# Scores of one attention group and values of another in one TensorE visit, with the second batch's probabilities turned by DMA

## The chip, the cores and the metric

The kernel runs on one core of a Trainium2 chip. The metric is the device time of one execution in microseconds (us). All times below come from runs of the kernel before and from one profiled execution of it.

## What is computed

The inputs are q, k and v of 8 batches, 8 heads, 576 tokens and 64 values a head, and two weight matrices. Attention is sparse: in the first four heads a query sees the last 32 tokens, in the other four those tokens before it that stand at the same place modulo 32. A feed-forward layer with a gate follows.

```python
def _attn_ref(q, k, v):                      # B, H, S, D = 8, 8, 576, 64
    scores = (1 / np.sqrt(D)) * np.matmul(q, k.transpose(0, 1, 3, 2))
    rel = pos[:, None] - pos[None, :]
    mask_local = (rel >= 0) & (rel < 32)
    mask_strided = (rel >= 0) & (pos[None, :] % 32 == pos[:, None] % 32)
    masks = np.stack([mask_local if h < H // 2 else mask_strided for h in range(H)])
    attn = softmax(np.where(masks, scores, -1e9))
    return np.matmul(attn, v)

def _moe_ref(x, w_in, w_out):                # x: 4608 x 512, w_in: 512 x 2048, w_out: 2048 x 512
    h = x @ w_in
    return (h / (1 + np.exp(-h))) @ w_out
```

## The kernel before

**Work.** The 4608 tokens form nine blocks of 512. Blocks 0 to 2 go through the feed-forward layer in the plain way: for each of 16 chunks of 128 hidden channels one step `h` (`hidden`, L676, twelve wide matmuls of 128x128 by 512 columns into a bank of the PSUM ring `ph`), then tanh (ACT, L692), gate (DVE, L696), a split of the result into a rounded and a remaining part (L705, L709), then one step `o` (`output`, L725, twelve wide matmuls into four `po` banks). Every product is made of three, since values are split in two. Blocks 3 to 8 go in three pairs through a scheme with seven products in place of eight (L1482 for the first layer, L1521 for the second), which accumulate in three PSUM tiles of two banks, z0 to z2. A step `A` or `B` of it is again twelve wide matmuls.

**Attention** lies between these steps. Batch 0 has six groups of its own (c = 0 to 5); each later batch has three (c = 6 to 26), each of them a local group of 12 tiles and a strided one of 8 or 6. For a group the steps are: `S` (`scores`, L503: small matmuls of 64 rows in two passes, 72 or 80 records), `M` (DVE: mask and maximum, L531), `E` (ACT: exponentials, L540), `R` and `N` (DVE: sums and scaling), then the probabilities are turned, then `O` (`values`, L607: again 72 or 80 small matmuls) and `B` (`placed`, L627: ACT copies from PSUM to the activations x). In batches 0 and 1 they are turned on TensorE (`T`, `turn`, L564, with ACT's copies `P`, L575). From batch 2 on (`MOVED`, L105) they are turned by DMA: `X` copies the upper and the lower 16-bit halves of the words apart (`part`, L591), `Y` is one DMA transpose (`move`, L597), `Z` joins the halves (`join`, L603). Of the batches from 1 on, scores, transposes and values all take the one PSUM ring `pa` (two banks). There is one buffer `pt` for turned probabilities, so a group's first `X` or `P` waits for the values of the group before.

**Order.** Nothing in the instruction streams is ordered by a compiler. Each step has a cost per engine, the steps that it follows, the rings that it takes (`ready`, L253) and a due time; `arrange` (L264) goes through time and each moment starts the step with the smallest due time among those that could start, choosing the engine that would end first. Due times come from the order in which steps are added (`backward`), and two tables written by hand correct them (`SHIFT`) or fix the engine (`GIVEN`). The result is one fixed order for each engine; PE, SP (which issues all DMAs), DVE, ACT and POOL then wait for one another by semaphores alone. `plan` (L992) says beside which chunk of blocks 1 and 2 values, turning and scores of a group are added, 3.55 chunks for each group; `spread` (L1654) does the same for the first pairs. Loads of weights pass through six stage buffers and are rounded by ACT and DVE up to some 126 us.

Of the kernel before, what the change touches and what calls it, by code (L numbers as in the profile page):

```python
# [30 lines left out]
P = 128  # L31
# [43 lines left out]
class Group:  # L75
# [29 lines left out]
MOVED = 2  # L105
# [68 lines left out]
}  # L174
GIVEN = {
# [4 lines left out]
}  # L180
# [1578 lines left out]
```

## Time and profile before

| | us |
|---|---|
| median of 3 runs (lowest, highest) | 818.92 (816.71, 820.82) |
| the profiled execution | 815.51 |
| its span, first to last instruction | 813.7 |
| PE busy | 801.4 (98% of the span) |
| DVE busy | 563.2 (69%) |
| ACT busy | 498.6 (61%) |
| POOL busy | 4.7 (1%) |
| packets of the main DMA queue, share of 16 engines | 70.5% |

Shares of busy time are means over stages that differ, so the rows further down come by stage. PE is the matmul engine. Matmuls overlap and their ends are modelled, so differences of starts are safer than durations. A line number belongs to the kernel before.

### The profile page before, as it was taken

The page shows a single profiled execution, that of the slowest core. Times are in us where ns is not written, and L with a number is a line of the kernel's source. Part 1 is how long each engine was busy: PE and PEld are TensorE (multiplying, and loading weights), DVE is VectorE, ACT ScalarE, POOL GpSimd, SP SyncE. Part 2 cuts the span into 40 slices and gives each one's busy share as a digit, 9 for nine tenths or more (in the row PEclk, how much of TensorE's full clock was granted, in tenths as well). Part 3 has the DMA queues.
Part 4 walks back from the last instruction along what each step waited for, and adds up shares of the span by engine and source line. Part 5 has one row for each costly group of instructions (what it writes and reads, how often), then busy time and mean ns, then how long its engine had stood idle before and what let it go on. Part 6 is the DMA issues. An engine that isn't in the chain of part 4 may idle for free.

```text
span 813.7 us, 17555 instructions
## 1 busy us (share of the span) xinstructions
PE 801.4 (98%) x6920; PEld 656.1 (81%) x6920; DVE 563.2 (69%) x1382; ACT 498.6 (61%) x1176; POOL 4.7 (1%) x24
## 2 busy tenths in 40 slices
PE   6999999999999999999999999999999999999997
PEld 4888888888888888888888888888888888888886
DVE  6989887578888789822798776227976640379662
ACT  7998877355786748755787764564544344445440
POOL 2000000000000000000000000000000000000000
PEclk9999999999999999999999999999999999999999
DMA  8998796787876776776788777765555665555662
GB/s 321 324 309 277 256 259 221 213 264 224 241 215 216 229 221 236 262 237 230 261 247 255 275 242 263 215 200 192 194 205 196 233 243 176 201 207 185 209 225 105
DMA packets 107362, 188.85 MB, mean 232 GB/s; under 512 B 37648, under 2 KB 81680, under 8 KB 96528
## 3 DMA queue, kind: packets, MB, share of 16 engines
q1 hardware_dynamic: 107280, 187.74, 70.5%
q8 instruction: 54, 0.88, 0.4%
q14 instruction: 28, 0.23, 0.1%
HBM read 141.05 MB, written 38.80 MB: 221 GB/s over the span
## 4 chain that ended last, share of the span: by engine, by line
PE 97%; DVE 1%; DMA 1%; ACT 0%; issue 0%; SPq 0%; DVEq 0%
PE z L1482 28%; PE z L1521 28%; PE ph L682 17%; PE po L729 16%; PE pa L512 3%; PE pa L621 3%; DMA w<-kqt 1%; PE pa L569 0%; DVE osb L531 0%; PE po L621 0%; DVE sm L531 0%; DVE osb L548 0%; DVE osb L562 0%; DVE sums L557 0%; PE po L512 0%
## 5 line engine op out<-in xcount | busy, mean ns | idle before, releaser
L1482 PE MATMUL z<-w,w 128*128 128x512 f32 x720 | 167.1, 391 | 0.0
L1482 PEld LDWEIGHTS z<-w,w 128*128 128x128 f32 x720 | 134.5, 188 | 28.2
L1521 PE MATMUL z<-w,w 128*128 128x512 f32 x576 | 134.4, 390 | 0.0
L682 PE MATMUL ph<-xhi,w 128*128 128x512 f32 x384 | 127.8, 396 | 0.0
L1521 PEld LDWEIGHTS z<-w,w 128*128 128x128 f32 x576 | 107.8, 188 | 22.5
L540 ACT ACTIVATE sm<-sm,sums 128x64 f32<-128x64 f32 x304 | 101.7, 339 | 26.9 <-DVE sums L531 26.6
L729 PE MATMUL po<-w,g 128*128 128x512 f32 x432 | 103.7, 392 | 0.0
L729 PEld LDWEIGHTS po<-w,g 128*128 128x128 f32 x432 | 80.3, 188 | 17.0
L1348 DVE TENSOR_TENSOR w<-w,w 128x1024 fp32r<-128x1024 f32 (+3 forms) x68 | 77.5, 1151 | 11.1 <-ACT w L1419 9.4
L682 PEld LDWEIGHTS ph<-xhi,w 128*128 128x128 f32 x384 | 72.0, 188 | 15.9
L682 PE MATMUL ph<-xlo,w 128*128 128x512 f32 x192 | 74.8, 390 | 0.0
L1377 DVE TENSOR_TENSOR w<-w,z 128x1024 f32<-128x1024 f32 x30 | 36.5, 1219 | 43.2 <-PE z L1482 43.2
L1419 ACT CAST w<-w 128x1024 fp32r<-128x1024 f32 (+1 forms) x40 | 39.2, 987 | 32.9 <-PE z L1521 32.0
L540 ACT ACTIVATION_READ_ACCUMULATOR sm<-sm,sums 128x1 f32 x304 | 58.0, 191 | 0.0
L1365 ACT ACTIVATE w<-w 128x1024 f32<-128x1024 f32 x30 | 31.8, 1060 | 37.1 <-DVE w L1377 36.9
L1521 PE MATMUL z<-xhi,w 128*128 128x512 f32 x216 | 52.0, 390 | 0.0
L1521 PE MATMUL z<-xlo,w 128*128 128x512 f32 x216 | 52.0, 390 | 0.0
L1371 ACT COPY w<-z 128x1024 f32<-128x1024 f32 x30 | 30.4, 1013 | 34.7 <-PE z L1482 34.6
L1521 PEld LDWEIGHTS z<-xlo,w 128*128 128x128 f32 x216 | 40.5, 188 | 8.5
L1521 PEld LDWEIGHTS z<-xhi,w 128*128 128x128 f32 x216 | 40.5, 188 | 8.4
L692 ACT ACTIVATE th<-ph 128x512 f32<-128x512 f32 x48 | 28.5, 594 | 25.5 <-PE ph L682 13.5
L682 PEld LDWEIGHTS ph<-xlo,w 128*128 128x128 f32 x192 | 36.1, 188 | 6.9
(159 smaller groups left out, 1134.8 us busy)
## 6 DMA issues: line engine op xcount, KB each, us to landing
w<-ops SPq DMA_DIRECT2D x84, 1024.0 KB, 4.9
ops<-stage SPq DMA_DIRECT2D x48, 256.0 KB, 2.9
kd<-kqt SPq DMA_DIRECT2D x24, 448.0 KB, 5.1
ops<-w SPq DMA_DIRECT2D x80, 128.0 KB, 4.0
vd<-vt SPq DMA_DIRECT2D x24, 384.0 KB, 5.5
stage<-w_in SPq DMA_DIRECT2D x16, 512.0 KB, 6.2
stage<-w_out SPq DMA_DIRECT2D x16, 512.0 KB, 5.0
kd<-kqt SPq DMA_DIRECT2D x14, 442.0 KB, 4.6
```

Source lines behind the costliest of these rows:

```text
L512: nc.tensor.matmul(self.pss[rows, r, at : at + KW], kd[half, 1, g.q0[t] : g.q0[t] + g.rows], kd[half, 0, g.k0[t] : g.k0[t] + KW], start=Tr ...
L540: nc.scalar.activation(out=self.s_sb[:, c, r], in_=self.s_sb[:, c, r], func=AF.Exp, bias=self.nmax[:, c, r : r + 1], scale=-1.0, accum_out ...
L682: nc.tensor.matmul(ph, weight(0, wi, fc)[:, cc * P : (cc + 1) * P], x[xi][:, cc], start=(cc, n) == (0, 0), stop=(cc, n) == (NP - 1, 2),)
L692: nc.scalar.activation(out=th[:, cols], in_=ph[:, cols], func=AF.Tanh, scale=0.5)
L729: nc.tensor.matmul(po[tt], g[gi][:, cols], weight(1, wi, fc), start=fc == 0 and n == 0, stop=fc == NFC - 1 and n == 2,)
L1348: nc.vector.tensor_tensor(out=o, in0=x, in1=y, op=op1)
L1365: nc.scalar.activation(out=o, in_=x, func=AF.Silu)
L1371: nc.scalar.copy(out=o, in_=x)
L1377: nc.vector.tensor_add(o, x, y)
L1419: nc.scalar.copy(out=hi, in_=x)
L1482: nc.tensor.matmul(zt[z][:, jj], w[:, at, wi, cc * P : (cc + 1) * P], op[:, xi, cc], start=fresh and (cc, n) == (0, 0), stop=(cc, n) == (1 ...
L1521: nc.tensor.matmul(zt[zz][:, ds], w[:, at, wi, ds * P : (ds + 1) * P], op[:, gi, jj], start=fresh and (jp, jj, n) == (0, 0, 0), stop=(jp, ...
```

## The change

Five things are changed together:

1. From c = 9 to c = 24 the values of group c and the scores of group c + 2 are one step `V` for PE: first all of the scores, then all of the values, with nothing between them (`add_both`). These are 16 steps. Scores still go to `pa`. Values go to both banks of the ring `ph` in blocks 1 and 2 (nine steps), and to one of the tiles z0 to z2 in the first two pairs (seven steps). The last two groups keep a values step of their own.
2. Where values are in `ph`, ACT copies the local group in two instructions (one for each bank) in place of one.
3. Behind such a step in blocks 1 and 2 the output step of the same chunk is added at once.
4. `MOVED` is 1: batch 1 too is turned by DMA. Three `T` with their `P` go, three groups of `X`, `Y` and `Z` come.
5. `X` and `Z` may be done by POOL as well as by DVE or ACT; the planner chooses, and `GIVEN` names a few. Planned costs of these steps are other ones.

The tables `SHIFT` and `GIVEN` are new as a whole, and steps of one kind follow each other in the order of their chunks (`prior`).

```diff
-MOVED = 2
+MOVED = 1
...
-    copy = {"DVE": nc.vector.tensor_copy, "ACT": nc.scalar.copy}
+    copy = {"DVE": nc.vector.tensor_copy, "ACT": nc.scalar.copy, "POOL": nc.gpsimd.tensor_copy}
...
-        def values(self):
-            self.pso = self.bank("pso")
+        def values(self, ring=None):
+            if ring == "ph":
+                self.pso = [ps.tile([P, T], F32, name="ph") for _ in range(2)]
+            else:
+                at = pools["ps2"].tile([P, 2, T], F32, name=ring) if ring else self.bank("pso")
+                self.whole_pso, self.pso = at, [at[:, b] for b in range(2)]
...
+                if self.split:
+                    for b in range(2):
+                        nc.scalar.copy(
+                            out=flat[:, x0 + b * n : x0 + (b + 1) * n], in_=self.pso[b][:, base : base + n]
+                        )
+                    return
...
+    def add_both(c, ring):
+
+        a, s = groups[c], groups[c + 2]
+        a.split = ring == "ph"
+        add_keys(c + 2)
+        add_vs(c)
+
+        def go():
+            s.scores()
+            a.values(ring)
+
+        v = do(f"V{c}", {"PE": 2.68}, go,
+               reads=[f"kd{k}" for k in s.k] + [f"vd{v}" for v in a.v]
+               + [f"pt{c}.{i}" for i in range(len(a.gs))],
+               writes=[f"pss{c + 2}", f"pso{c}"], takes=[s.ring("pss")] + [ring] * (1 + a.split))
...
-                x = do(f"X{c}.{half}", {e: 0.1 + 0.13 * a.n for e in ("DVE", "ACT")}, lambda: None,
-                       reads=parts, writes=[f"half{c}.{half}"], due=after(0), takes=[] if half else [a.pt_from],
-                       after=[steps[f"X{c}.0"]] if half else [])
+                x = do(f"X{c}.{half}", {"POOL": 0.2 + 0.14 * a.n, "DVE": 0.06 + 0.08 * a.n, "ACT": 0.1 + 0.12 * a.n},
+                       lambda: None, reads=parts, writes=[f"half{c}.{half}"], due=after(0),
+                       takes=[] if half else [a.pt_from], after=[steps[f"X{c}.0"]] if half else before(c))
...
-        for what, c, at in (("V", i, 3.55 * i), ("T", i + 1, 3.55 * i + 1.2), ("S", i + 2, 3.55 * i + 2.4)):
+        for what, c, at in (("B", i, 3.55 * i), ("T", i + 1, 3.55 * i + 1.2)):
...
+                if plan[k, fc][0][0] == "B" and fc < NFC - 1:
+                    add_output(k, fc)
+                    put_out.add((k, fc))
...
-    for i, when in enumerate(((1, 2, 3), (4, 5, 6), (8, 9, 11), (13, 16, 18), (21, 23, 25), (29, 31, 33))):
-        spread(0, late + i, when)
-    for i, when in enumerate(((1, 2, 3), (5, 6, 7), (9, 10, 11))):
-        spread(1, late + 6 + i, when)
+    for i, when in enumerate(((2, 4, "z2"), (6, 8, "z1"), (10, 12, "z2"), (13, 16, "z0"), (20, 22, "z2"), (28, 30, "z1"))):
+        spread(0, late + i, *when)
+    for i, when in enumerate(((13, 15, "z2"), (21, 23), (29, 31))):
+        spread(1, late + 6 + i, *when)
```

## Rows read from the trace of the kernel before

**Rows 1.** table of stages: start:end, length, busy PE, PEld, DVE, ACT, POOL, clock, DMA share, GB/s

```profile
0.00:26.20 26.20, 18.18 (x485) 14.37 (x485) 18.71 (x110) 20.11 (x73) 4.74 (x24) 1.00 0.92 327
26.20:126.00 99.80, 99.80 (x1094) 81.48 (x1094) 89.97 (x279) 86.51 (x259) 0.00 (x0) 1.00 0.89 281
126.00:330.00 204.00, 204.00 (x2258) 165.63 (x2251) 165.99 (x553) 131.16 (x426) 0.00 (x0) 1.00 0.75 229
330.00:581.00 251.00, 251.00 (x2096) 205.79 (x2096) 153.55 (x316) 163.04 (x318) 0.00 (x0) 1.00 0.72 236
581.00:809.50 228.50, 228.46 (x1008) 188.88 (x1007) 133.73 (x126) 97.79 (x103) 0.00 (x0) 1.00 0.56 200
```

**Rows 2.** chain that ended last, in order of time: start us, us, what

```profile
140.10 1.32 PE pa L621 x80
...
156.62 2.72 PE ph L682 x12
...
217.06 1.32 PE pa L621 x80
```

**Rows 3.** timeline of PE around a scores visit: start us, us, line, operation, tiles, shapes

```profile
226.38 0.39 PE L682 MATMUL ph<-xhi,w 128*128 128x512 f32 x1
226.69 1.35 PE L512 MATMUL pa<-kd 64*32 64x64 f32 x80
227.97 0.50 PE L682 MATMUL ph<-xhi,w 128*128 128x512 f32 x1
...
228.54 0.40 PE L682 MATMUL ph<-xhi,w 128*128 128x512 f32 x1
```

**Rows 4.** groups by line, shapes apart: scores on 64x64 tiles; busy us, mean ns

```profile
L512 PE MATMUL pa<-kd 64*64 64x64 f32 x616 | 13.8, 225 | 0.0
```

**Rows 5.** timeline of PE around a values visit

```profile
124.11 0.84 PE L729 MATMUL po<-stage,g 128*128 128x512 f32 x3
124.89 1.39 PE L621 MATMUL pa<-pt,vd 64*64 64x32 f32 x80
...
126.54 0.40 PE L682 MATMUL ph<-xlo,w 128*128 128x512 f32 x1
```

**Rows 6.** timeline of PE in the opening, values ahead of scores

```profile
25.15 0.44 PE L621 MATMUL po<-th,w 64*64 64x54 f32 x13
25.83 0.44 PE L621 MATMUL po<-th,w 64*64 64x54 f32 x11 [0.24 <-issue]
```

**Rows 7.** page, DMA queues: packets, MB, share of 16 engines

```profile
q8 instruction: 54, 0.88, 0.4%
```

**Rows 8.** timeline of PE around the transposes of the first group of batch 1

```profile
39.66 0.39 PE L682 MATMUL ph<-xhi,w 128*128 128x512 f32 x1
39.90 0.93 PE L569 MATMUL pa<-ident,sm 128*128 128x128 f32 x7
...
41.12 0.40 PE L682 MATMUL ph<-xhi,w 128*128 128x512 f32 x1
```

**Rows 9.** instructions on tile pt: count, ns lowest/median/highest, first and last start us

```profile
L605 ACT COPY pt<-sm x23: 1059/1201/1225, 122.8 to 542.4; 128x896 uint16<-128x896 uint16 x16, 128x768 uint16<-128x768 uint16 x7
...
L595 DVE COPY pt<-sm x16: 554/620/628, 107.4 to 536.3; 128x896 uint16<-128x896 uint16 x10, 128x768 uint16<-128x768 uint16 x6
```

**Rows 10.** groups by line on POOL: busy us, mean ns

```profile
L368 POOL COPY mask_first<-mask_local 128x72 f32<-128x72 f32 x2 | 0.5, 238 | 0.1
```

**Rows 11.** DMA issues: count, median us from issue to landing

```profile
sm<-pt SPq DMA_TRANSPOSE x18, 4.5
```

**Rows 12.** timeline of ACT behind a values visit, ACT idle before

```profile
141.48 0.93 ACT L650 COPY xb<-pa 128x144 f32<-128x144 f32 x3 [2.76 <-PE pa L621]
142.19 0.54 ACT L633 COPY xb<-pa 128x384 f32<-128x384 f32 x1
```

**Rows 13.** timeline of ACT behind a values visit, ACT busy

```profile
223.72 0.54 ACT L633 COPY xb<-pa 128x384 f32<-128x384 f32 x1
```

**Rows 14.** timeline of ACT ahead of the first group turned by DMA

```profile
122.77 1.21 ACT L605 COPY pt<-sm 128x896 uint16<-128x896 uint16 x1
```

More of the change, by code (lines that the diff above doesn't have):

```diff
@@ L255, in ready @@
         at = 0.0
-        for ring in step.takes:
-            if len(self.taken[ring]) >= self.rings[ring]:
-                for other in self.taken[ring][-self.rings[ring]].ends[ring]:
+        for i, ring in enumerate(step.takes):
+            back = self.rings[ring] - step.takes[:i].count(ring)
+            if len(self.taken[ring]) >= back:
+                for other in self.taken[ring][-back].ends[ring]:
                     if other.end is None:
@@ L758, in sparse_attention_ffn, with add_keys @@
     outs_of = {}
+    def add_keys(c, after=lambda d: None):
+        a = groups[c]
+        for g, gi, k in zip(a.gs, a.gis, a.k):
+            cols = max(g.nq, g.nk)
+            do(f"k{c}.{gi}", {"SP": 2 * P * cols * 4 / QUICKER}, lambda gi=gi, k=k: load_qk(a.b, gi, k),
+               writes=[f"kd{k}"], due=after(-6))
+    def add_both(c, ring):
[10 more added lines that the diff above has]
+               writes=[f"pss{c + 2}", f"pso{c}"], takes=[s.ring("pss")] + [ring] * (1 + a.split))
+        both.append(v)
+        if not a.split:
+            late_steps.append(v)
+        add_peaks(c + 2, v)
+        take_values(c, v, ring)
+        add_total(c + 2)
+    both = []
     def add_scores(c, t0=None):
@@ L801, in add_total, with before @@
         steps.ends(steps[f"M{c}.0"], "sum", [r])
+    def before(c):
+        return [steps.by_name[n] for n in (f"O{c - 1}", f"V{c - 1}") if n in steps.by_name]
     def add_turn(c, t0=None):
@@ L818, in add_turn @@
             for half in range(2):
-                z = do(f"Z{c}.{half}", {e: 0.1 + 0.13 * a.n for e in ("DVE", "ACT")}, lambda: None,
-                       reads=parts, writes=[f"pt{c}.{half}"], due=after(0))
+                z = do(f"Z{c}.{half}", {"POOL": 0.2 + 0.14 * a.n, "DVE": 0.06 + 0.09 * a.n, "ACT": 0.12 + 0.157 * a.n},
+                       lambda: None, reads=parts, writes=[f"pt{c}.{half}"], due=after(0))
                 z.act = lambda z=z, half=half: a.join(half, z.engine)
@@ L835, in add_turn, with add_vs @@
         steps.ends(steps[f"M{c}.0"], a.sm_from, [t])
+    def add_vs(c, after=lambda d: None):
+        a = groups[c]
+        for g, gi, v in zip(a.gs, a.gis, a.v):
+            do(f"v{c}.{gi}", {"SP": P * g.count * D * 4 / QUICKER}, lambda gi=gi, v=v: load_v(a.b, gi, v),
+               writes=[f"vd{v}"], due=after(-5))
     def add_values(c, t0=None):
@@ L840, in add_values @@
         ring = a.ring("pso")
[L841 to L843 removed]
+        add_vs(c, after)
         o = do(f"O{c}", {"PE": 1.46 if a.b else 1.5 if a.gs[0].local else 1.05}, a.values,
@@ L846, in add_values, with take_values @@
                writes=[f"pso{c}"], takes=[ring], due=after(0))
+        return take_values(c, o, ring, after)
+    def take_values(c, o, ring, after=lambda d: None):
+        a = groups[c]
         steps.ends(steps[f"X{c}.0" if a.moved else f"P{c}.0"], a.pt_from, [o])
@@ L849, in add_values @@
         for i, (g, gi) in enumerate(zip(a.gs, a.gis)):
-            x = do(f"B{c}.{i}", {"ACT": 0.53 if g.local else 0.75}, lambda i=i: a.placed(i),
+            x = do(f"B{c}.{i}", {"ACT": (0.66 if a.split else 0.53) if g.local else 0.75}, lambda i=i: a.placed(i),
                    reads=[f"pso{c}"], due=after(1 + i / 2))
@@ L902, in sparse_attention_ffn, with prior @@
     lows = [x_steps(0, cc, done[cc], 22 + cc)[1] for cc in range(NP)]
+    def prior(name, fc):
+        return [steps[f"{name}{fc - 1}"]] if fc else []
     def chunk_steps(fc):
@@ L998, in attend @@
     def attend(events):
-        for what, c in events:
+        for what, c, *ring in events:
             if c >= len(groups):
                 continue
-            if what == "V":
+            if what == "B":
+                add_both(c, *(ring or ["ph"]))
+            elif what == "V":
                 add_values(c)
@@ L1132, in add_output @@
         o = do("o" + name, {"PE": 2.72}, go, reads=[("w", 1, fc)] + ([f"gl{name}"] if k else []),
-               after=[split_at[1, fc]] + ([] if k else [made[fc][2]]),
+               after=[split_at[1, fc]] + ([] if k else [made[fc][2], steps[f"o{fc - 1}"]]),
                writes=[("po", tt) for tt in range(NTT)])
@@ L1652, in sparse_attention_ffn, with spread @@
     at = [{}, {}, {}]
-    def spread(p, c, when):
-        for what, n, step in zip("VTS", range(3), when):
-            at[p].setdefault(step, []).append((what, c + n))
-    for i, when in enumerate(((1, 2, 3), (4, 5, 6), (8, 9, 11), (13, 16, 18), (21, 23, 25), (29, 31, 33))):
-        spread(0, late + i, when)
-    for i, when in enumerate(((1, 2, 3), (5, 6, 7), (9, 10, 11))):
-        spread(1, late + 6 + i, when)
+    def spread(p, c, first, second, ring=None):
+        at[p].setdefault(first, []).append(("B", c, ring) if ring else ("V", c))
+        at[p].setdefault(second, []).append(("T", c + 1))
+    for i, when in enumerate(((2, 4, "z2"), (6, 8, "z1"), (10, 12, "z2"), (13, 16, "z0"), (20, 22, "z2"), (28, 30, "z1"))):
+        spread(0, late + i, *when)
+    for i, when in enumerate(((13, 15, "z2"), (21, 23), (29, 31))):
+        spread(1, late + 6 + i, *when)
     until = len(steps.all)
@@ L1668, in sparse_attention_ffn @@
     changed.behind += [step for step in steps.all[mark:until] if inside.match(step.name)]
+    for v in both:
+        if v.takes[-1] == "ph":
+            changed.behind += [v, *v.ends["ph"]]
     for step in late_steps:
@@ L1680, in sparse_attention_ffn @@
                 step.after += [steps[f"h{SINGLE - 1}.{fc}"] for fc in range(5)]
+    for v in both:
+        for step in v.ends[v.takes[-1]]:
+            v.after += [s for s in step.after if s is not v and s not in v.after]
     steps.backward(mark, 125.0)
+    for v in both:
+        for i, step in enumerate(v.ends[v.takes[-1]]):
+            step.due = v.due + 2.7 + i / 2
     for name, shift in SHIFT.items():
```

34 lines of the change are left out of this document (17 added, 17 removed), and 104 rows, old and new, of tables (GIVEN, SHIFT).

## The prediction

> **What bounds the kernel now.** I read the table of stages first. From 26.2 us to 809.5 us TensorE (PE) is busy 783.3 us of 783.3: 99.80 of 99.80, 204.00 of 204.00, 251.00 of 251.00 and 228.46 of 228.50 [rows 1]. Before that it idles 26.20 - 18.18 = 8.0 us, and the span of 813.7 us leaves 4.2 us behind 809.5 for the last store. The granted clock is 1.00 everywhere, the upper of the two levels (2.4 GHz). So the kernel is one long row of TensorE work, and a microsecond of it that goes is a microsecond of span, as long as nothing else comes late. DVE is nearest to doing so: 90.0 of 99.8 us up to 126, then 166 of 204, 154 of 251; ACT 86.5, 131, 163; the DMA engines 0.89, 0.75, 0.72; POOL does nothing behind 26.2 us [rows 1]. The second view is the chain that ended last: it alternates blocks of twelve wide matmuls, 2.72 us, so 0.227 us each, with attention visits of 1.2 to 1.3 us [rows 2]. I read a visit's price from the starts of the wide matmuls around it, because the ends of matmuls are modelled.
>
> **Merged visits.** Around a scores visit the last wide matmul starts at 226.38 and the third behind it at 228.54; three at 0.227 would take 0.68, so the visit costs 2.16 - 0.68 = 1.48 us. Its 80 starts take 1.35 less the last one's 0.22, 1.13 us; 0.35 us is entering and leaving [rows 3]. A values visit: the last of three wide ones starts at 124.11 + 0.84 - 0.39 = 124.56, the second behind at 126.54: 1.98 - 0.45 = 1.53 us, its starts 1.39 - 0.22 = 1.17 us, so 0.36 us of changing over [rows 5]. Values right behind scores keep their 1.17 us and lose the 0.36, less what the hand-over costs. No such pair stands in the trace. Lower bound 0.015 us, the pace inside a visit (1.17 us over 79). Upper bound 0.15: in the scores visit the last small start is 227.82, and the next wide one 227.97 [rows 3]. I take 0.04, near the lower end: the last scores are strided ones on 64x64 tiles [rows 4], values begin on 64x64 tiles [rows 5], and inside the values visit the step from local to strided group is within the pace. 16 x (0.36 - 0.04) = 5.1 us; by the upper bound 3.4. The Trainium skill (TensorEngine Tiling (Array Packing), Key Properties) says that changing the tiling mode, not just the tile, drains TensorE; here the mode stays, so by it the hand-over is the cheap one, and the sum with a drain would be the 3.4. No row shows this hand-over itself.
>
> **A cost in the merged visit.** It issues some 80 + 80 weight loads and matmuls in a row, 320 instructions in 2.4 us. Just once the trace has a similar density, values of two groups and then scores from 24.2 us; there PE sits idle for 0.24 us behind the 13th strided matmul with "issue" as its reason, and from start to start (25.15 + 0.44 - 0.22 = 25.37 to 25.83) it is 0.46 us [rows 6]. The instruction queue fetched 0.88 MB in 54 packets [rows 7], and 6920 matmuls with as many weight loads are 13840 instructions, some 256 in a packet: a lone visit (160) spans at most one edge between packets, a merged one (320) can span two. My estimate: a gap of 0.46 us where two edges fall into one visit, (320 - 256) / 256 of 16 = 4 visits, some of them covered: 1.0 us. Ends 0 and 16 x 0.46 = 7.4.
>
> **Transposes of batch 1.** Three visits go: 39.66 to the third wide matmul behind at 41.12 is 1.46 - 0.68 = 0.78 us for seven transposes [rows 8]; twice that and 0.66 for six by the same pace: 2.2 us. Added: four 16-bit copies and one DMA transpose a group. On DVE a first copy is 0.62 us, on ACT a second one 1.20 [rows 9]; twelve at some 0.9 are 11 us; the six copies from PSUM that go are left out. DVE and ACT have 9.8 + 13.3 us free up to 126 [rows 1], and POOL all of it. POOL's nearest row copies 72 columns in 0.238 us [rows 10]; in proportion 896 would be 2.96 us; below stands DVE's 0.62; I take 1.2, the longer of ACT's, since it is the same form. Each sits in a chain between two TensorE visits, not on TensorE. The DMA transposes land in 4.5 us [rows 11]. One moves 0.46 MB, at the stage's 281 / 0.89 = 316 GB/s 1.5 us of all engines, so three take 4.4 to 13.5 us of the 11 us that the DMA engines have left up to 126; I take the low end, as other transfers ran meanwhile: nothing. In SP's queue weight loads stand behind each transpose and wait with it for its copies; the ring of six stages hides that while PE has rounded weights ahead. At the high end PE loses 2.5 us.
>
> **Where values land.** Nine merged visits now take both ph banks, the ones of the hidden chunks. So both gates before must be done, and no hidden chunk starts till ACT has copied out both banks. What is queued behind on PE is one output chunk, which the diff appends there, 2.72 us [rows 2]. A values visit ends at 140.10 + 1.32 = 141.42 with ACT idle; its copies end at 142.19 + 0.54 = 142.73, 1.3 us later [rows 2, 12]. With ACT busy, the visit ending 218.38 has its last copy ending at 223.72 + 0.54 = 224.26, 5.9 us later [rows 2, 13]. Nobody waited, since the bank pa was not wanted. The split local copy adds a fixed part, some 0.3 us. If ACT serves these copies first, 1.6 us lie under 2.72 and it costs 0; I take 0.5 us in all, for a few late ones. The seven later visits use a free z bank that nothing else wants in those steps: nothing. Scores keep pa, which transposes and most values leave: below nothing is possible in waits, but PE has none to give back after 26.2 us. In the first 26.2 us the new due times move work among 8.0 us of idle; with nothing there that the change touches I take 0, ends -2 and +1.
>
> **Sum.** The profiled execution took 815.51 us (span 813.7): 815.5 - 5.1 - 2.2 + 1.0 + 0.5 = 809.7 us. The median of the runs is 818.92, 3.4 above it, so on that scale 813.1 us. What is late next is still TensorE.
>
> **The rivals.** *Fetch gaps in every merged visit:* 5.1 + 2.2 - 7.4 = -0.1 given back fully, so 818.9, no change. For it stands the one gap [rows 6], against it that most visits would need two packet edges. *PE waits for the two ph banks (the slower side):* the price is (delay of the last copy - 2.72) x 9. At 5.9 it is 29 us, at the mean of the two rows, 3.6 + 0.3 with the split copy, 1.2 x 9 = 11 us: 818.9 - 7.3 + 11 = 822.6. It decides from 3.5 us of delay on, where 0.8 x 9 eats the 7.3. For it speaks ACT's 131 of 204 us of work in that stage, against it that the copies can be put first in ACT's order. *POOL gets in DVE's way or DVE in POOL's:* if a POOL copy advances only while DVE is idle, 1.2 us becomes 1.2 / 0.19 = 6.3 us up to 330, two of them lengthen a chain by 10 us. The first such chain has 0.9 us in hand (the copy ends at 123.98, values start at 124.89) [rows 5, 14]. At 1 us lost per visit in that stage, some nine visits, 818.9 - 7.3 + 9 = 820.6; no instruction of POOL behind 26.2 us says for or against. The Trainium skill (GPSIMD Engine Reference, Key points) has POOL share its SBUF interfaces with VectorE, with contention where DVE works in a two-port mode or reads two SBUF inputs; this speaks for it, and no run here shows it. *The order in the opening gains:* 811. *It does not do what it says*, scores and values separated or transposes still there: the code joins them in one step, so little, and 818.9.
>
> **How the numbers follow.** A measurement of this kernel can tell about 0.5% (4.1 us) from no change: below 814.8 is faster, above 823.0 slower. Forecast 0.57 (some of its upper part falls into the same); opening 0.05; fetch gaps 0.14; port 0.08; ph banks 0.13; not done 0.03. Faster 0.58, the same 0.25, slower 0.17. The range: all of 5.1 + 2.2 + 2 off gives 809.6, rounded to 809.0 for the runs' own spread; upward 820.0 takes in the fetch gaps and the DMA bound and leaves out most of the ph and port cases, somewhat under 2 in 10.
>
> **What would show it.** Right: between two wide matmuls around a merged visit some 2.7 us more than the pace, no wait at the hand-over, L569 in batch 0 alone, PE still busy without a break behind 26.2 us, POOL busy 20 us or more, last ph copies within 2.7 us of a visit. Wrong: "issue" gaps inside merged visits; PE waiting behind an output chunk for ACT's copies; POOL copies of 3 us and more with PE waiting for pt.

## The result and the profile after

The change makes the kernel slower: 824.22 us median of 12 runs (820.45 to 828.38) beside 818.14 of the kernel before on the same chip, ratio 1.008, 95% interval [1.0057, 1.0103]. A second sample of the same engine streams (e_z9late, below) gave 1.0037 [1.0019, 1.0055]; the two intervals do not meet, so ratios of separate comparisons can be set against each other to some 0.4% only. The forecast was 813.1 us. The profiled execution took 823.39 us, its span is 821.5 us; the one of before, 815.51, lies at the low end of that kernel's runs, so the two traces stand 7.9 us apart and the medians 6.1.

The table of stages of the changed kernel, in the stretches and columns of [rows 1]:

```profile
0.00:26.20 26.20, 16.15 (x508) 13.21 (x508) 17.44 (x109) 19.37 (x69) 4.74 (x24) 1.00 0.91 327
26.20:126.00 99.80, 94.44 (x951) 75.50 (x950) 86.22 (x238) 79.82 (x226) 10.30 (x9) 0.97 0.83 249
126.00:330.00 204.00, 201.00 (x2068) 165.03 (x2068) 167.41 (x509) 108.20 (x380) 27.42 (x24) 0.99 0.77 234
330.00:581.00 251.00, 250.24 (x2212) 207.03 (x2202) 162.84 (x381) 164.84 (x373) 22.89 (x19) 1.00 0.77 244
581.00:809.50 228.50, 228.50 (x1149) 189.03 (x1148) 139.87 (x131) 103.13 (x114) 1.07 (x1) 1.00 0.59 207
```

TensorE no longer works without a break behind 26.2 us: it lacks 5.4 us up to 126, 3.0 us up to 330, 0.8 us up to 581, and its granted clock has left 1.00 in two stages. GpSimd has 62 us of work that it had not.

The merged visit is as forecast. TensorE around scores of 72 and values of 80 (timeline, columns as in [rows 3], which shows a lone scores visit; [rows 5] a lone values visit):

```profile
281.76 1.75 PE L743 MATMUL po<-w,g 128*128 128x512 f32 x7
283.44 1.23 PE L516 MATMUL pa<-kd 64*32 64x64 f32 x72
284.50 1.34 PE L629 MATMUL ph<-pt,vd 64*64 64x32 f32 x80
285.76 2.60 PE L743 MATMUL po<-w,g 128*128 128x512 f32 x10
```

By the starts of the single matmuls the third wide one behind the visit begins 3.22 us after the last one ahead of it: 2.54 us for the visit. Apart they cost 1.37 (72 scores) and 1.53 (80 values), so one entry saves 0.36 us, 16 of them 5.8. The first values start 0.04 us behind the last scores, as taken; there both work on 64x64 tiles. Inside each scores visit the step from 64x32 to 64x64 tiles takes 0.15 us. The Trainium skill (TensorEngine Tiling (Array Packing), Key Properties) has a drain at a change of the tiling mode alone; the trace agrees, with these 0.04 and 0.15 us. The three transposes of batch 1 [rows 8] are gone. So the 7.3 us of forecast gain are there (8.0 by these starts), and some 14 to 16 were lost elsewhere. Three kinds of place show where. The opening, TensorE (before, the first wide matmul started at 27.48; here at 33.98):

```profile
24.81 0.68 PE L516 MATMUL pa<-kd 64*64 64x64 f32 x27 [1.99 <-issue]
...
28.69 1.22 PE L516 MATMUL pa<-kd 64*32 64x64 f32 x68 [1.59 <-DVE sums L535]
32.52 0.58 PE L516 MATMUL pa<-kd 64*64 64x64 f32 x10 [2.61 <-issue]
```

The scores of group 7, 1.5 us, now stand ahead of the first wide matmul; they wait for their bank, and twice TensorE has no instruction for 2 to 2.6 us. Next, a wait ahead of the second 512 tokens:

```profile
132.44 0.50 PE L696 MATMUL ph<-xlo,w 128*128 128x512 f32 x1 [1.69 <-DVE xlo L688]
```

The granted clock behind these waits (windows; columns as in [rows 1]):

```profile
30.70:33.90 3.20, 1.38 (x44) 1.36 (x44) 1.47 (x3) 0.38 (x3) 0.00 (x0) 0.50 0.88 249
34.00:37.40 3.40, 3.40 (x10) 2.72 (x9) 2.13 (x8) 3.28 (x12) 0.00 (x0) 0.50 0.83 280
37.60:41.00 3.40, 3.40 (x16) 2.78 (x15) 1.78 (x4) 1.90 (x8) 0.00 (x0) 1.00 0.24 56
130.00:132.40 2.40, 0.75 (x3) 0.19 (x1) 2.40 (x3) 2.40 (x14) 1.96 (x2) 1.00 1.07 380
133.10:136.50 3.40, 3.40 (x10) 2.65 (x9) 3.30 (x7) 2.20 (x13) 0.00 (x0) 0.50 1.01 354
```

0.50 is the lower level, 1.2 GHz. It follows stretches in which TensorE had stood; ten or so wide matmuls then run 0.43 apart, 1.6 to 1.8 us lost each time. Last, a gap inside a merged visit:

```profile
234.22 1.32 PE L629 MATMUL ph<-pt,vd 64*64 64x32 f32 x74
236.85 0.33 PE L629 MATMUL ph<-pt,vd 64*64 64x54 f32 x6 [1.31 <-issue]
```

### The profile page after: what moved, and what is told of

It reads as the page before. It is cut to its first block, busy times and chain, and to the rows that moved or that the text cites. A ratio compares the mean times of both kernels' runs of the same rounds, so it can differ in the third digit from the quotient of the medians.

```text
span 821.5 us, 17632 instructions
## 1 busy us (share of the span) xinstructions
PE 797.9 (97%) x6900; PEld 655.7 (80%) x6900; DVE 575.1 (70%) x1365; ACT 475.4 (58%) x1159; POOL 66.4 (8%) x77
## 4 chain that ended last, share of the span: by engine, by line
PE 90%; DMA 4%; DVE 3%; issue 1%; ACT 1%; POOL 0%; SPq 0%; DVEq 0%; ACTq 0%; POOLq 0%
PE z L1583 28%; PE z L1544 26%; PE ph L696 15%; PE po L743 14%; PE pa L516 3%; DMA stage<-w_out 2%; DMA sm<-pt 1%; PE ph L629 1%; PE z L629 1%; DMA w<-kqt 1%; DVE sm L535 0%; PE po L629 0%; PE pa L629 0%; PE ph L573 0%; DVE stage L413 0%
## 5 line engine op out<-in xcount | busy, mean ns | idle before, releaser
L1439 DVE TENSOR_TENSOR w<-w,z 128x1024 f32<-128x1024 f32 x30 | 36.5, 1218 | 33.0 <-PE z L1544 32.9
L599 POOL COPY pt<-sm 128x896 uint16<-128x896 uint16 (+1 forms) x30 | 31.0, 1054 | 342.0 <-DVE sums L535 124.3
L609 POOL COPY pt<-sm 128x896 uint16<-128x896 uint16 (+1 forms) x23 | 30.6, 1343 | 207.5 <-DMA sm<-pt 198.5
```

Source lines behind the costliest of these rows:

```text
L599: copy[engine](out=to[:, half], in_=self.halves(self.sm)[:, half])
L609: copy[engine](out=self.halves(self.pt)[:, half], in_=came[:, half])
L1439: nc.vector.tensor_add(o, x, y)
```

## The experiments

Each kernel ran beside the kernel before on its chip; kernels with the same time before ran side by side, and their medians compare directly. "Wide" below is the start of the n-th wide matmul of 512 columns (two of 256 count as one), by which traces of different orders compare.

| kernel | median us | before us | ratio, 95% interval |
|---|---|---|---|
| changed | 824.22 | 818.14 | 1.0080 [1.0057, 1.0103] |
| e_more208 | 827.43 | 819.43 | 1.0100 [1.0076, 1.0124] |
| e_act | 827.12 | 819.43 | 1.0096 [1.0065, 1.0128] |
| e_split | 845.00 | 819.43 | 1.0320 [1.0295, 1.0346] |
| e_vfirst | 832.45 | 819.43 | 1.0169 [1.0137, 1.0200] |
| e_s7late | 823.35 | 820.13 | 1.0047 [1.0028, 1.0066] |
| e_z9late | 822.61 | 820.13 | 1.0037 [1.0019, 1.0055] |
| e_halves | 827.75 | 820.13 | 1.0098 [1.0082, 1.0115] |
| e_three | 827.29 | 820.13 | 1.0092 [1.0070, 1.0113] |
| e_graft | 819.05 | 818.99 | 0.9999 [0.9984, 1.0014] |
| e_tail | 833.04 | 818.99 | 1.0179 [1.0163, 1.0195] |
| e_first | 823.53 | 818.99 | 1.0064 [1.0040, 1.0087] |
| e_opening | 828.01 | 819.33 | 1.0118 [1.0097, 1.0139] |
| e_turn21 | 815.42 | 819.33 | 0.9959 [0.9944, 0.9975] |
| e_best | 814.62 | 819.33 | 0.9955 [0.9937, 0.9972] |
| e_best2 | 816.44 | 818.78 | 0.9972 [0.9959, 0.9985] |
| e_pool | 817.33 | 818.78 | 0.9982 [0.9963, 1.0000] |
| e_first_act | 825.08 | 818.78 | 1.0087 [1.0065, 1.0108] |

**Instruction fetch: e_more208.** The third scores visit of the opening repeats 52 pairs of its matmuls:

```diff
     def scores(self):
         self.pss = self.bank("pss")
+        self.score_matmuls()
+        if (self.b, self.gis) == (0, (2,)):
+            for n in (24, 24, 4):
+                self.score_matmuls(n)
```

> The changed kernel, with 52 of the matmuls of the third scores visit issued again at its end (208 more TensorE instructions at about 6 us, where TensorE waits for a load anyway; results unchanged). Theory of the instruction fetch: TensorE's waits with the reason issue (2.0 us at 24.8, 2.6 us at 32.5, 1.3 us at 236.9 in the changed kernel) fall where its stream crosses into a packet of 256 instructions that has not come yet; all edges now lie 208 instructions earlier in the work, so those three waits go or move, the sum of issue waits in the opening falls from 4.6 us to 2 us or less, the half clock at 30.7 to 37.5 us goes with them, and the time falls by 3 to 7 us (816 to 821 where the changed kernel has 824). Rival, the order of the work: the waits stand at the same matmuls as before and the time stays within 1.5 us.

Counted along TensorE's own stream (a matmul and its weight load are two instructions, and its semaphore instructions count too), the "issue" gaps of the changed kernel fall at instructions 961, 1217, 5312 and 9665; here at 448, 1217 and 1472. All are 192 or 193 above a multiple of 256, in every kernel below too, and none stays with its matmul. So the location is settled: a gap is the end of a packet of 256 instructions. That the next packet is still on its way shows in the transfers of the instruction queue. Ahead of the end of the gap at 236.85 in the changed kernel it moved one (DMA queues: packets, MB, share; window 234.5 to 235.6):

```profile
q8 instruction: 1, 0.02, 5.5%
```

These 16,384 bytes ran from 234.58 to 235.55, and the gap ended 1.3 us later. All 50 such gaps of the nineteen traces end 1.2 to 1.6 us behind the end of a transfer of this size. The time went the other way, though (827.4 where 816 to 821 was forecast): 1.97, 1.52 and 1.26 us of gaps in the opening in place of 2.20 and 2.83, and 1.5 us of added matmuls. Gaps inside merged visits disappeared (one of 1.00 us stands right behind a visit), and just one visit still holds two ends of packets.

**e_act, e_split, e_vfirst: three parts of the rest.** GpSimd's copies made by ScalarE at the same places; values one step of TensorE behind the scores; values ahead of scores:

```diff
+        if step.engine == "POOL" and step.name[0] in "XZ":      # e_act
+            step.engine = "ACT"
...
-            s.scores()                                          # e_split: a.values(ring)
-            a.values(ring)                                      # one TensorE step later
...
-            s.scores()                                          # e_vfirst
-            a.values(ring)
+            a.values(ring)
+            s.scores()
```

> The changed kernel in its own order, but every copy that POOL makes is made by ACT at the same place in the order. Theory of the shared ports: DVE instructions with two SBUF inputs that lie beside a POOL copy take 1.34 us where they take 0.69 alone, about 12 us of DVE time in all, some of it ahead of TensorE's wait at 130 to 132 us; without POOL none of them is over 0.75 us, DVE busy falls from 575 to about 563 us, that wait shrinks to 1 us or less, and the time falls by 1 to 4 us. Rival, ACT's load: 57 us more of copies on ACT (475 to some 535 us busy) delay its exponentials and its copies out of PSUM, and the time rises by 2 to 8 us although DVE's instructions are short.

> The changed kernel in its own order, but in each of the 16 joined visits the values are issued one TensorE step (twelve or six wide matmuls) later than the scores. Theory of the saved changeover: each pair costs some 2.90 us where it costs 2.54 to 2.64 joined, 16 x 0.36 = 5.8 us more work, and the three issue waits inside joined visits (2.9 us) go, so the time rises by about 3 us (826 to 828). Rival, joining is worth nothing in the end, since waits take it back: the time stays within 1 us or falls.

> The changed kernel with the order inside the 16 joined visits turned round: values, then scores. Theory of the drain between tile shapes: the hand-over from 64x64 tiles of the values to 64x32 tiles of the local scores takes 0.15 us where that from 64x64 to 64x64 takes 0.02 to 0.04, so a joined visit takes some 2.65 us instead of 2.54 and the time rises by 16 x 0.11 = 1.8 us; a little may come back because the PSUM banks of the values are copied out earlier. Rival, no such drain: joined visits stay at 2.54 us and the time within 1 us.

e_act: VectorE's busy time falls by 18 us, and nothing is gained in sum. One wait goes: the two subtractions ahead of TensorE's wait at 132.44 are short without GpSimd's copies (timelines of VectorE, changed kernel, then e_act):

```profile
129.76 2.62 DVE L688 TENSOR_TENSOR xlo<-xb,xhi 128x64 fp32r<-128x64 f32 x2 [0.48 <-ACT xhi L683]
```

```profile
129.22 0.23 DVE L688 TENSOR_TENSOR xlo<-xb,xhi 128x64 fp32r<-128x64 f32 x1 [0.92 <-ACT xhi L683]
129.69 0.63 DVE L688 TENSOR_TENSOR xlo<-xb,xhi 128x448 fp32r<-128x448 f32 x1 [0.24 <-ACT xhi L683]
```

The wait falls from 1.69 to 0.2 us, and no half clock follows. But ScalarE has 45 us more work, and TensorE's waits pass to gates and weights (waits of PE in the whole span of e_act: engine, line, releaser, us in sum, times, longest):

```profile
PE ph L696 <- DVE th L710: 3.2, 5, 1.2
PE po L743 <- DVE stage L449: 1.6, 1, 1.6
PE z L629 <- ACT pt L609: 0.9, 1, 0.9
PE ph L696 <- ACT w L449: 0.7, 1, 0.7
```

e_split costs 20 us more than the changed kernel, far above its forecast. With the output chunk between scores and values, nothing covers the copies of the two ph banks (timeline of PE):

```profile
161.62 3.02 PE L743 MATMUL po<-w,g 128*128 128x512 f32 x12
164.57 1.39 PE L629 MATMUL ph<-pt,vd 64*64 64x32 f32 x80
167.02 0.50 PE L696 MATMUL ph<-xhi,w 128*128 128x512 f32 x1 [1.06 <-ACT xb L664]
```

So the output chunk behind the joined visit does hide them, and in this order joining is worth more than its 0.36 us. e_vfirst: a joined visit without a gap costs 2.68 in place of 2.54 us, about as forecast, 2.3 us in 16. The whole lost some 7 us by the ratios, far more than the forecast 1.8; for most of the rest stand gaps within visits, 0.86, 2.08 and 3.42 us, where the changed kernel has 1.53 and 0.28.

**Four edits of places: e_s7late, e_z9late, e_halves, e_three.** In the finished order, a step and what needs it is put behind another; and wide matmuls are made in two halves, to shift the ends of packets without new columns:

```diff
+    later(["S7"], "i1")                    # e_s7late, e_three
+    later(["Z9.0", "Z9.1"], "h1.3")        # e_z9late, e_three
...
-                    ph, weight(0, wi, fc)[:, cc * P : (cc + 1) * P], x[xi][:, cc],
+                    ph[:, cols], weight(0, wi, fc)[:, cc * P : (cc + 1) * P], x[xi][:, cc, cols],
```

> The changed kernel with one step moved in the finished order: the scores visit of group 7 (the first of batch 1 to use the second key buffer; 1.5 us of TensorE) stands behind the second wide half chunk pair (behind i1) and no longer between the values of groups 5 and 4, and what reads its scores follows it. Nothing else is changed. Theory A (the opening lost its time because one more visit of small matmuls was put ahead of the first wide matmul: TensorE waited 1.59 us for the bank of that visit, stood 2.61 us without an instruction in its middle, and made its 1.5 us of matmuls): the issue gap at 29.7 to 32.5 us is gone, the values of group 4 start when their transposed scores are there (ScalarE's copy ends at 29.75), so the first wide matmul comes at 30.8 to 31.3 us in place of 33.98; the visit itself is paid later, 1.5 us; net gain 1.5 us of waiting and issue gap at least, and up to 1.8 us more if the half clock of 30.7 to 37.6 us goes with the gaps. Total 819.5 to 822.0 us where the changed kernel had 824.2. Theory B (the opening is set by DMA and the vector work, TensorE's order is only where it shows): the first wide matmul stays at 33 us or later, or the gain comes back as a wait before 60 us, total 823 to 826 us.

> The changed kernel with two steps moved in the finished order: GpSimd's two copies of the transposed scores of group 9 (at 129.66 and 130.78 us, beside the subtraction that makes the low part of the input's third quarter for the next 512 tokens) stand some 14 us later, behind h1.3; they are read at 163 us at the earliest. Theory A (the shared way to SBUF: the two subtractions took 1.31 us each beside the copies, 0.35 each where GpSimd was idle, and TensorE waited 1.69 us for them, then ran 3.4 us at half clock): the two subtractions take 0.7 to 0.8 us together, TensorE's wait at 130 us falls from 1.69 to 0.3 or less, the clock holds there, total 3 us less by the wait and the clock, so 820.5 to 822.5 us. Theory B (the subtraction is late because its engine and ScalarE are late by the weights, which run 4.2 to 4.4 us apart): the subtractions are short but TensorE waits next for ScalarE's high part or for a weight piece, by 1 us or more, total 823.0 to 825.0 us.

> The changed kernel with 105 of the wide matmuls of chunks h1.1 to h1.5 (from 131 us) made as two of 256 columns each, which gives the same sums and takes the same columns; it adds 210 instructions to TensorE's stream there, so that every later packet of 256 instructions ends at another matmul. Theory A (issue gaps come where two ends of packets lie close together in a run of small matmuls): the gaps at 235.3 (1.53), 411.6 (0.92) and 437.9 us (0.38) are gone, none of over 0.5 us appears from 150 us on, as with 208 more instructions in the opening; the halves cost nothing to 1 us (each half brings a weight load, 0.11 us of matmul over it), total 821.0 to 823.0 us. Theory B (the gaps belong to these visits, whatever the position): they stay, total 824 to 826 us.

> The three edits together: the scores visit of group 7 behind i1, GpSimd's two copies of group 9 behind h1.3, and 105 wide matmuls in halves. If the three losses are separate and are what I hold them to be, their gains add: 824.2 less 2.5 (opening), less 2.5 (wait and clock at 130 us), less 2.5 (issue gaps in merged visits) is 816.7 us, range 814 to 819, faster than the kernel before (818 to 819) by 0 to 0.6%. If one gain is given back at the next wait, the sum is short by it: 819 to 822 us.

e_s7late: the first wide matmul comes at 31.68 (forecast 30.8 to 31.3), and the gap in that visit is gone, but at 41.76 TensorE waits 1.70 us for a gate. The 121st wide matmul starts at 65.1, in the changed kernel at 64.7: theory B. e_z9late did nothing: GpSimd has no work ahead of these copies, so a later place in the program starts them no later, and they stand at 132.23 beside the subtraction as before. It is a second sample of the changed kernel. e_halves: I had counted twelve matmuls to a chunk as twenty-four, so the halves lie at 270 to 327 us, behind the gap at 235, which stayed; the one at 437.9 went, another of 0.85 us came at instruction 9920, and a wait of 1.88 us for GpSimd's copy at 376.7 with half clock behind it. A pair of halves costs some 13 ns (500 wide matmuls around them took 132.0 us, 130.6 in the changed kernel). e_halves and e_three came out slower than either of their theories, by some 5 us against e_z9late, which ran beside them. What is repaired in one place of the front comes back at the next.

**Grafts: e_graft, e_tail, e_first.** A finished order is a list of steps with engines, so an order can be joined of two. Nothing else changes.

```diff
-    for step in steps.arrange():
-        step.act()
+    for name, engine in listed:            # e_graft: before up to 125.5 us, then changed
+        named[name].engine = engine        # e_tail: changed up to 126 us, then before
+    for name, engine in listed:            # e_first: before up to 39 us, then changed
+        named[name].act()
```

> One part of the change alone, the later one: the steps that the kernel before begins in its first 125.5 us by its plan stand here in its order and on its engines (batch 1 turned by TensorE, no GpSimd copy, its opening), and everything behind stands as in the changed kernel (16 merged visits, values in ph and z banks, GpSimd copies). Theory A (the merged part is worth its 5 us and more, and the loss lies ahead of 126 us): the first wide matmul at 27 to 28 us and no half clock before 137 us as in the kernel before, the stretch behind as in the changed kernel with up to 3 us of issue gaps; total 811 to 815.5 us, ratio 0.991 to 0.996. Theory B (the merged visits and what serves them give their gain back by themselves, by issue gaps and waits for GpSimd's copies): total 817 to 821 us.

> The other part alone: the steps that the changed kernel begins in its first 126 us by its plan stand in its order and on its engines (its opening, batch 1 turned by DMA with GpSimd copies), and everything behind as in the kernel before (scores and values in visits of their own, copies by ScalarE and VectorE). Theory A (the loss lies ahead of 126 us; it is 12 us between the two plans and the merged visits hide a part): first wide matmul at 33 to 35 us, waits near 107 and 130 us, half clock at two places, total 824 to 829 us, ratio 1.007 to 1.012, which is slower than the changed kernel or as slow, though it has none of its merged visits. Theory B (the loss belongs to the merged part): total 815 to 820 us.

> The changed kernel with the opening of the kernel before: the steps that the kernel before begins in its first 39 us by its plan stand in its order and on its engines; everything behind as in the changed kernel, with batch 1 turned by DMA and the merged visits. Theory A (two losses of like size, one in the opening and one at 96 to 136 us by the copies and the moved weights): first wide matmul at 27 to 28 us and no half clock at 31 to 38 us, so 6 to 8 us earlier there, but waits of 3 to 5 us at 100 to 136 us as in the changed kernel; total 816 to 819 us. Theory B (the opening's lead is given back by 136 us, as the weights' chain sets that stretch): TensorE reaches the second 512 tokens (128 us in the changed kernel) less than 3 us earlier than there; total 821 to 825 us. Theory C (batch 1 by DMA costs nothing once the opening is as before): the lead is kept whole, total 813 to 816 us.

| wide | 1st | 121st | 241st | 361st | 481st | end |
|---|---|---|---|---|---|---|
| before | 27.5 | 58.7 | 91.7 | 122.1 | 153.7 | 813.7 |
| changed | 34.0 | 64.7 | 96.7 | 128.7 | 160.0 | 821.5 |
| e_graft | 30.3 | 62.2 | 95.2 | 125.7 | 153.7 | 819.1 |
| e_first | 30.2 | 63.1 | 97.6 | 129.1 | 158.4 | 819.9 |
| e_tail | 32.9 | 63.8 | 95.9 | 127.0 | 170.5 | 830.6 |
| e_best | 29.8 | 61.1 | 94.1 | 124.6 | 152.3 | 812.8 |

The front of the kernel before with the merged rest takes 819.05, in theory B's range: the merged part does not bring its gain by itself. The changed front costs 0.4 to 0.8% over it. e_first shows that taking the opening back does not undo the front's loss: with the old opening 3.8 us are won at the first wide matmul, and by the 361st nothing is left. Waits of TensorE in e_first (timeline):

```profile
50.76 0.47 PE L812 MATMUL ph<-xhi,w 128*128 128x512 f32 x1 [1.37 <-ACT w L565]
72.93 0.47 PE L812 MATMUL ph<-xhi,w 128*128 128x512 f32 x1 [1.20 <-DVE th L826]
...
132.42 0.50 PE L812 MATMUL ph<-xlo,w 128*128 128x512 f32 x1 [1.55 <-DVE xlo L804]
```

These are waits for weights, gates and the input's low part, the work of VectorE and ScalarE. e_tail is no clean measure: from the 361st to the 481st wide matmul it loses 12 us more against before, at its seam, where values wait up to 2.9 us for copies that each order had placed elsewhere.

Behind the front, e_graft shows two stalls. One is a turn that came late. Timelines of SP, of GpSimd and of TensorE:

```profile
393.89 6.57 SPq L717 DMA_TRANSPOSE sm<-pt  x1
```

```profile
405.61 2.26 POOL L724 COPY pt<-sm 128x896 uint16<-128x896 uint16 x1 [13.97 <-DMA sm<-pt]
```

```profile
407.92 2.40 PE L744 MATMUL z<-pt,vd 64*64 64x32 f32 x80 [2.45 <-POOL pt L724]
```

Issued right behind a weight load of 1 MB, its data came 11.6 us after the issue (the other seventeen: 3.4 to 7.1); the clock is 0.50 up to 413.8. The changed kernel has the same late turn (10.9 us) and 0.70 us of wait. The other stall stands at the end of a merged visit:

```profile
349.67 1.34 PE L744 MATMUL z<-pt,vd 64*64 64x32 f32 x80
352.54 3.02 PE L1659 MATMUL z<-xhi,w 128*128 128x512 f32 x12 [1.53 <-ACT xb L779]
```

The profile names ScalarE's copy, but these matmuls write another bank, and the gap begins at instruction 7873, again 193 above a multiple of 256, and ends 1.4 us behind a transfer of 16,384 bytes.

**Away with these two: e_opening, e_turn21, e_best.**

```diff
-    ... u12 E22.1 ... E22.6 Y21 ...        # e_turn21, e_best: the turn of group 21 issued
+    ... Y21 E22.1 ... E22.6 u12 ...        # ahead of the weight load u12
...
+                halved = not ends and FROM <= next(passed) < FROM + 24    # e_best: 48 instructions more
...
+    # e_opening: changed up to 39 us, then before up to 125.5 us, then changed
```

> The opening of the changed kernel alone: the steps that it begins in its first 39 us by its plan stand in its order and on its engines; then, up to 125.5 us, the order of the kernel before, with batch 1 turned by TensorE; then the merged visits as in the changed kernel. The run with the whole front of the kernel before and this rest took 819.05, the run with the front's opening from before and batch 1 by DMA 823.5. Theory A (the two parts of the front each cost about half, and what the opening loses stays lost): 821.5 to 824 us. Theory B (the opening's loss is given back by 126 us, as other engines are the bound there): 818 to 820.5 us, first wide matmul at 33 us but the second 512 tokens begun at 126 to 127 us as without it. Theory C (the opening is the whole loss): 824 us or more.

> The kernel with the front of the kernel before and the merged visits of the changed one (819.05), with one DMA issue moved: the turn of group 21 (its two loads' neighbours on SP's queue) is issued ahead of a 1 MB weight load and no longer behind it. There its data came 11.7 us after the issue, where the other seventeen took 3.6 to 7.8, GpSimd's copy of it took 2.26 us, TensorE stood 2.45 us for it and then ran 3.4 us at half clock. Theory A (that place is worth the wait and the clock): the turn takes 5 to 8 us, no wait at 405 us, no half clock there, 4 us less: 814.5 to 816.5 us. Theory B (the slow turn is a matter of the DMA rings' load, not of the order): the wait stays at 1.5 us or more, 818 to 820 us.

> The same with the turn of group 21 ahead of the weight load, and 24 wide matmuls of two hidden chunks ahead of the visit of group 16's values made as two of 256 columns, so that 48 more instructions move the packet end that fell two instructions ahead of the end of the visit of group 18 (1.53 us without an instruction at 350.8). Theory A (both losses are what I hold them to be): 1.4 us less than with the moved turn alone, 813 to 815.5 us, ratio to the kernel before 0.993 to 0.996. Theory B (the gap comes back at another visit): as with the moved turn alone.

e_turn21 gains 0.4% on e_graft, within its range. Two separate comparisons of the same streams differed by as much; that the place is worth it is seen in the trace, where the data now comes 6.1 us after the issue and both the wait of 2.45 us and the half clock are gone. The same turn in e_best, timelines of SP and of GpSimd:

```profile
391.28 3.61 SPq L717 DMA_TRANSPOSE sm<-pt  x1
```

```profile
399.13 1.24 POOL L724 COPY pt<-sm 128x896 uint16<-128x896 uint16 x1 [8.40 <-DMA sm<-pt]
```

No wait follows, and the clock holds there. In e_turn21 the gap at the packet's end is still there, 2.03 us, with another releaser beside it; in e_best the visit runs through, and 1.41 us come back at instruction 8385, behind the next visit:

```profile
369.92 3.70 PE L1666 MATMUL z<-w,w 128*128 128x512 f32 x15 [1.02 <-issue]
```

So the 48 instructions moved a gap more than they removed one; 0.0004 of ratio between the two kernels is nothing that can be told. e_best is faster than both kernels: 0.9955 and, once more, 0.9972. e_opening is in theory C's range, but not for its reason: at the first wide matmul it stands where the changed kernel does (34.0), at the 361st 6.7 us behind it (135.4), with waits for a key load (1.84 us) and for copies (1.06 us) behind the seam. So the two parts of the front do not add up (e_first loses 4.5 us against e_graft, e_opening 9), and the opening's share is left open.

**Port or load: e_best2, e_pool, e_first_act.**

```diff
+        if name in beside:                 # e_pool: behind ten weight pieces
+            for at in range(0, 960, 192):
+                copy["POOL"](out=pad0.bitcast(U16), in_=weight(layer, 0, fc).bitcast(U16)[:, at : at + 192])
...
+    X6 to Z9: POOL -> ACT                  # e_first_act, on e_first
```

> The kernel of e_best once more, unchanged, beside the next two on one chip. Expected: ratio to the kernel before 0.993 to 0.998, 812.5 to 817 us.

> e_best with idle work for GpSimd in the front: behind the low part of ten weight pieces (42 to 112 us) GpSimd copies 128x960 halves of words of the finished piece, in five parts, into 384 bytes that nothing reads; some 13 us of copies, as many as batch 1's turn by DMA gives it in the changed kernel. Nothing waits for them except that a weight's place is not reused before it is read. Theory A (the copies slow VectorE's two-input and SBUF operations by their own length, and in the front VectorE has little idle time: 97 of 109 us busy between 27 and 136 us): mean times of the two-input operations there up by a tenth or more, TensorE waits in the front of 3 us or more in sum, total 817 to 821 us. Theory B (VectorE's slack takes it up): operations slower in the same way, but no waits of TensorE, total within 1 us of e_best. Theory C (GpSimd's copies of so few columns do not disturb VectorE): operations as in e_best.

> The kernel with the opening of the kernel before and batch 1 by DMA (823.5), with the eleven of batch 1's copies that GpSimd makes there made by ScalarE at the same places in the order. Theory A (GpSimd's copies beside VectorE are what batch 1's turn by DMA costs): VectorE's operations of 27 to 136 us at their usual lengths, waits at 50, 72 and 130 us smaller, total 819 to 821.5 us. Theory B (it is the load of the copies and the moved weights, whoever makes them): waits for ScalarE take the place, total 822.5 to 827 us.

VectorE's subtraction for the weights between 27 and 136 us, in e_best2 and then in e_pool (groups by line: busy us, mean ns, idle before):

```profile
L568 DVE TENSOR_TENSOR w<-stage,w 128x512 fp32r<-128x512 f32 x26 | 17.7, 686 | 0.8 <-ACT w L564 0.2
```

```profile
L568 DVE TENSOR_TENSOR w<-stage,w 128x512 fp32r<-128x512 f32 x26 | 18.8, 730 | 0.7 <-ACT w L564 0.2
```

The copies slow VectorE by 6% there and cost nothing that the intervals can tell, though GpSimd is busy with them for 29 us, and in e_first for 12.8. The real copies of e_first fall on other operations: the same subtraction takes 689 ns, but the cast of a weight piece 529, and 426 in e_first_act, where GpSimd is idle. Yet e_first_act is no faster: ScalarE is busy 96.9 of the 109 us in place of 87.7, and TensorE waits 2.43 us for its weights at 50 us and 1.17 for a gate at 87 us. Theory B, twice.

## Why the prediction was wrong

*What bounds the kernel now* was right for the trace, but it took the 9.8 and 13.3 us that VectorE and ScalarE had free up to 126 us [rows 1] as room. They were not, as far as e_s7late, e_first and e_first_act show: each time a wait was taken away, one for a weight or a gate came in its place. That the front is a chain in which each engine is nearly full is my reading of this, not shown by itself.

*Merged visits:* right. 5.8 us by the starts, forecast 5.1. From the 361st wide matmul to the end e_best, e_best2 and e_pool take 687.0 to 688.5 us, the kernel before 691.6: 3.1 to 4.6 of it arrive.

*A cost in the merged visit:* right in kind, too small in size. Two ends of packets in one visit do it, and five of the changed kernel's 16 visits hold two (estimated: 4). Only two of the five have a gap; what decides between them was not found. But a gap is 0.3 to 3.4 us and not the 0.46 of [rows 6]: 1.53 and 0.28 us in the changed kernel's visits, 1.8 in sum where 1.0 was taken, and 0.9 to 3.4 in e_vfirst's. The packet was estimated from [rows 7], and holds 256 instructions.

*Transposes of batch 1:* the step that failed first. The 2.2 us are gained, but "nothing" for what is added, with 2.5 at the high end, was wrong: against e_graft, which ran beside it, e_first, which has the old opening and turns batch 1 by DMA, is 4.5 us slower, and it has 2.2 us less to do. That is 6.7 of the 11.9 us between the forecast's -5.8 and the measured +6.1; e_first has a seam of its own at 39 us, whose cost is in it. Taking GpSimd's copies away does not bring it back (e_first_act), and such copies alone do not cost it (e_pool). What is left is the order of the front with five steps (X twice, Y, Z twice) in each group's chain; how the loss divides among them was not separated, so its mechanism stays open.

*Where values land:* right. The output chunk covers the copies; e_split shows the price without it, 1.06 us of wait a visit.

*The opening*, "I take 0, ends -2 and +1", was wrong in the trace: the first wide matmul came 6.5 us later, one scores visit, two gaps and a half clock. Its price in time stays open: e_s7late and e_first won 2.3 and 3.8 us there and had lost them by the 121st or 361st wide matmul, while e_opening, with this opening ahead of the old order, is 9 us above e_graft.

*What was not in the sum:* the turn that lands late behind a weight load, and the half clock behind each longer stall. e_turn21 puts the first with its clock at 0.4%, 3 to 4 us in e_graft; in the changed kernel its wait is 0.70 us. In the two traces the forecast is 13.6 us off. Up to the 361st wide matmul 6.7 us are lost where 2.2 should be won, 8.9 in all. Behind it 1.1 are lost where 3.6 should be won: the wait at 132.44 and its half clock are some 3.4 of these 4.7, the longer gaps 0.8, the late turn 0.7.

*The rivals:* none of them gives the whole. The port rival happened at one wait, the 1.69 us and the half clock at 132.44, 3.4 us, which went in e_act. Its rows: one subtraction of VectorE alone and beside a copy (timeline of VectorE, then of GpSimd, changed kernel):

```profile
117.18 0.69 DVE L723 TENSOR_TENSOR g<-th,g 128x512 fp32r<-128x512 f32 x1
...
121.50 1.42 DVE L723 TENSOR_TENSOR g<-th,g 128x512 fp32r<-128x512 f32 x1
```

```profile
121.39 0.99 POOL L599 COPY pt<-sm 128x896 uint16<-128x896 uint16 x1 [13.56 <-PE pa L629]
```

The Trainium skill (GPSIMD Engine Reference, Key points) has the two engines share their interfaces to SBUF, with contention where VectorE reads two SBUF inputs; the trace agrees, 0.69 us alone and 1.42 beside a copy. Elsewhere it decided little: nothing was gained in sum without the copies. The ph rival fell with its chunk in place. The range failed because it took the front as a place where nothing comes late.

## What to carry to other kernels

Where every engine is near full, a step that goes from the bounding engine to others is priced by what their chains then make late, and free time in a table of stages is no such price; a joined order of two schedules finds the guilty stretch faster than edits of single places. Issue a transfer that the bounding engine will wait for ahead of a large load on the same queue. Where many small instructions stand in a row, count them: two ends of packets of 256 close together can cost more than the visit saves.

## What the runs showed of the hardware

TensorE's stream comes in packets of 16 KB, 256 instructions; each gap with "issue" as its reason fell at instruction 192 or 193 of one and ended 1.2 to 1.6 us behind such a transfer, and the releaser named there can be a bystander. VectorE's operations with two inputs in SBUF, and its copies within SBUF, take longer beside a GpSimd copy (a subtraction 1.42 us in place of 0.69), those that read PSUM do not (684 ns before, 682 after, for the gate); GpSimd's copies stretch too, from 0.93 to 2.26 us. A DMA transpose landed 3.2 to 11.6 us after its issue; the longest, and 10.9, stood right behind a load of 1 MB.
